# A spectral filter block with a gated FFN on one core: the deferred tiles' half of the last evacuations, moved behind the inverse's first tile

## The chip, the cores and the metric

The kernel runs on one core of one Trainium2 chip. The metric is the device time of one execution in microseconds; several runs are taken and the median is given. The five instruction streams are TensorE (PE, with its weight loads as PEld), VectorE (DVE), ScalarE (ACT), GpSimd (POOL) and SyncE (SP). Each runs its own instructions in order, and they wait for each other by semaphores.

## The reference, cut to what matters

```python
x = A_x                                              # [1, 2048, 576] bf16
X = rfft2(layernorm(x)) * (w_r + 1j * w_i)           # over tokens and channels
h = x + irfft2(X, s=(2048, 576)).astype(bf16)
h2 = h + (gelu(layernorm(h) @ w_gate) * (layernorm(h) @ w_up)) @ w_down
return h2                                            # gate, up: 576x4608, down: 4608x576
```

## The kernel before

The 2048 tokens lie as 16 tiles of 128 tokens (token 16p + c is row p of tile c). The Fourier transforms are matmuls with tables.

**The forward part** handles 16 frequency groups, numbered i = 0 to 15 (GORD gives the place g of each). Its order is the hand-written word list SEQF (L28): D and d are the two passes of the channel transform, B the second token factor, T the multiplication by the filter on DVE, V and v the two passes of the first inverse token factor. The filter's last 32 channels (the remainder) of four groups are put together and go through R and r, q = 0 to 3. `st_V` (L686) evacuates a group's 128x512 results from a PSUM bank pair into V, by ACT and DVE or by one of them (VENG, L29); the last group, V15, is split between both. `st_R` (L702) evacuates the remainders. For q below 3 one copy goes to RB, and eight DMAs, split over SP's and POOL's queues, bring them to their rows in VR. For q = 3, the last, eight copies of 32 partitions x 128 elements write VR directly, four on ACT and four on DVE (L722 to L727). V has the token tile as its third index; VR has it as the last, so the weights of one tile are taken at a step of 16 elements.

**The inverse part** handles 16 token tiles. Tiles 0 to 7 go right away, in the order of the word list SEQ (L35): I and i are the two passes of the inverse channel transform (`i_mm`, L833; V in both, VR in the last step of the second pass), E its evacuation to GS (`i_ev`, L842; letter A, D, P or S for ACT, DVE, POOL or both), N and o the two passes of the last token factor (`n_mm`, L850), a the residual add on DVE (`x_add`, L859), s the sum of squares (L917), q and c the root and the reciprocal (L868, L873), n the normalisation (`norm`, L885, on POOL for tiles 0 to 3), u and U the transposes on PE (L901), e their evacuation, G the first two FFN steps. SEQ begins `I0 I1 I2 i0 E0S i1 E1S i2 E2A N0 I3 o0`. Tiles 8 to 15 are deferred: `def_i` (L991) and `def_n` (L1011) put their matmuls between those of the FFN, from f = 3 on.

**What sets the order.** Each engine's stream is just the order of the calls. PSUM is eight banks, used as four pairs in this stage. A small planner (L813 to L829) walks SEQ and gives each I, N and u the free pair that was used longest ago:

```python
if k in "INu":
    b = min((b for b in range(2 * ing, 4) if b not in held), key=lambda b: last[b])
```

The starting order comes from SEQF: the pair of V15 (banks 4 and 5) and that of R3 (banks 6 and 7) were used last. So I0 and I1 get the two other pairs, I2 that of V15, and N0 that of R3. The class Prog (L190) turns the keys that an operation reads and writes into waits: a matmul into a bank waits for every earlier reader of that bank.

**DMA queues.** SP loads tables, filter rows and the FFN weights; a call of `hold` (L762) lets SP wait for PE's position before a weight load (`loads`, L779: after I0, N0, i3, o1, N3, i7, o3). POOL issues the filter copies, its share of the remainders, and later the FFN weights.

**The FFN** takes four token blocks: 36 steps of gate and up (`gu_part`, L935: 18 matmuls, GELU on ACT, product on DVE), then the down projection (L1042), and the output.

Of the kernel before, what the change touches and what calls it, by code (L numbers as in the profile page):

```python
# [4 lines left out]
BF16 = mybir.dt.bfloat16  # L5
# [26 lines left out]
RENG = ['dve', 'act', 'act', 'act', 'act']  # L32
QR = ((0, 1), (1, 2), (2, 3), (3, 4), (4, 8), (8, 16))
DEF0, DSTEP = 3, 4
SEQ = """I0 I1 I2 i0 E0S i1 E1S i2 E2A N0 I3 o0 i3 N1 I4 o1 a0 E3S N2 o2 a1 s0A q0 i4 a2 s1A I7 c0 N3 E4S q1 s2D i7 I6 o3 E7A i6 c1 N4 o4 a3 q2 E6A c2 N7 I5 o7 a4 n0P N6 s3A a7 i5 n1P n2P q3 c3 o6 u1 U1 u2 E5A u0 U2 a6 n3P e1A e2D U0 N5 u3 e0A o5 a5 U3 G0 e3D G1""".split()  # L35


def _np_bf16(a):
# [8 lines left out]
def build_tables():  # L47
# [7 lines left out]
    T = {}  # L55
# [96 lines left out]
    T["BTAB"] = BN.reshape(128, 2 * 2 * 128)  # L152
    VN = VN.reshape(2, 2, 128, 256)
    assert np.allclose(VN[0, 0], VN[0, 1])
    T["VTAB"] = np.stack([v if k else v.reshape(128, 4, 16, 4).transpose(0, 1, 3, 2).reshape(128, 256) for v, k in ((VN[0, 0], 1), (VN[0, 0], 0), (VN[1, 0], 1), (VN[1, 1], 1), (VN[1, 0], 0), (VN[1, 1], 0))], 1).reshape(128, -1)

    kr = np.arange(1, K2)
    ph2 = ang(np.arange(2 * HK), kr).T
# [173 lines left out]
def _build(nc, A_x, A_w_r, A_w_i, B_w_gate, B_w_up, B_w_down, out):  # L332
# [76 lines left out]
    YS = sb.alloc("YS", [128, NY, 2, KW], BF16)  # L409
    TP = sb.alloc("TP", [128, NZ, 2, 2, 256], BF16)  # L410
    TR = sb.alloc("TR", [128, 2, 2, 2, 128], BF16)
    RB = sb.alloc("RB", [128, 3, 2, 2, 4, NT], BF16)

    GS = sb.alloc("GS", [128, 5, 2, KW], BF16)
    sb.off = v_off
# [14 lines left out]
    P.op(POOL, lambda g: g.memset(EPT[:, :], EPS), w=["EPT"])  # L430
    P.op(POOL, lambda g: g.memset(ZD[:, :], 0.0), w=["ZD"])
    P.op(POOL, lambda g: g.memset(EXQ[:, :], -0.5), w=["EXQ"])
    P.op(POOL, lambda g: g.memset(VR[:, :, :, :, :], 0.0), w=[("V", g, 2 + t) for g in range(NG) for t in range(2)])
    xv = A_x[0].rearrange("(p c) d -> p c d", c=NT)
    ov = out[0].rearrange("(p c) d -> p c d", c=NT)
    tabs = dram["ATAB"].rearrange("p (c k) -> p c k", c=NT)
# [178 lines left out]
    def ev(eng, dst, src, r, w):  # L615
        fn = (lambda v: v.tensor_copy(dst, src)) if eng == DVE else (lambda a: a.activation(dst, src, ACTF.Copy))  # L616
        P.op(eng, fn, r=r, w=w)
# [68 lines left out]
    def st_V(i, second, engs):  # L686
        g, z, b0 = GORD[i], i % NZ, FB["V", i]

        def mm(h, o, ct, first, last, after):
            c, t_ = ct  # L690
            return P.op(PE, lambda t: t.matmul(bank(b0 + o, 0, 128, 128 * c, 128 * c + 128), TP[64 * h:64 * h + 64, z, o, t_, c:256:2], VT[64 * h:64 * h + 64, 0 if g else 2 + o, t_, :],  # L691
                                               start=first, stop=last), r=[("T", z), "VT" if g else "VT2"], w=[("PS", b0 + o)], after=after)

        halves(("V", i), second, [[(c, t_) for c in range(2) for t_ in range(2)]] * 2, mm)
        if not second:
            return
        v5 = V[:, :, :, :, g, :, :].rearrange("p c t n j e -> p j (c t n) e")
        n = 2 // len(engs)
        for a, e in enumerate(engs):
            ev(e, v5[:, n * a:n * a + n], banks(b0 + a, n, 256).rearrange("p a (c e) -> p a c e", e=4), [("PS", b0 + a + k) for k in range(n)], [("V", g, a + k) for k in range(n)])  # L700

    def st_R(q, second):  # L702
        js = range(4 * q, 4 * q + 4)
        b0 = FB["R", q]

        def mm(h, o, pt, first, last, after):
            part, t_ = pt
            return P.op(PE, lambda t: t.matmul(bank(b0 + o, 0, 128, 128 * part, 128 * part + 128), TR[64 * h:64 * h + 64, q % 2, o, t_, :], VT[64 * h:64 * h + 64, 4 + o if part else 1, t_, :], start=first, stop=last),
                        r=[("TR", q % 2, j) for j in range(4)] + ["VT2" if part else "VT1"], w=[("PS", b0 + o)], after=after)

        halves(("R", q), second, [[(part, t_) for part in range(1 + (q == 3)) for t_ in range(2)]] * 2, mm)
        if not second:
            return
        keys = [("PS", b0), ("PS", b0 + 1)]
        if q < 3:
            ev(RENG[q], RB[:, q, :, :, :, :].rearrange("p t o e n -> p o t (e n)"), banks(b0, 2, 128).rearrange("p o (t x) -> p o t x", t=2), keys, [("RB", q)])
            for j, i in enumerate(js):
                for t_ in range(2):
                    k = t_ if q == 2 else (2 * j + t_) % 3 > 0
                    P.dma((SP, POOL)[k], VR[64 * t_ + 32 * (j % 2):64 * t_ + 32 * (j % 2) + 32, GORD[i], :, :, :], RB[32 * j:32 * j + 32, q, t_, :, :, :], f"r{q}{k:d}", r=[("RB", q)], w=[("V", GORD[i], 2 + t_)])  # L720
            return
        for i in js:  # L722
            j, g = i % 4, GORD[i]
            for t_ in range(2):
                dst = VR[64 * t_ + 32 * (j % 2):64 * t_ + 32 * (j % 2) + 32, g, :, :, :].rearrange("p o e n -> p o (e n)")
                src = PS[32 * j:32 * j + 32, b0 * 512:(b0 + 2) * 512].rearrange("p (a c) -> p a c", a=2)[:, :, 128 * (i == LAST) + 64 * t_:128 * (i == LAST) + 64 * t_ + 64]
                ev((ACT, DVE, DVE, ACT)[j], dst, src, keys, [("V", g, 2 + t_)])  # L727

    def dup_w(k, jp, pl=slice(0, 2), eng=None):
        a, b = 64 * jp, 64 - 64 * jp  # L730
# [19 lines left out]
    c = 0  # L750
# [56 lines left out]
    vmain = [("V", g, c) for g in range(NG) for c in range(2)]  # L807
    vtail = [("V", g, c) for g in range(NG) for c in range(2, 4)]
    vk = [vmain, vmain, vtail]
    vkeys = vmain + vtail  # L810


    SLOT, last, held, ing = {}, [sorted(used.values()).index(used[2 * b]) - 4 for b in range(4)], set(), False  # L813
    for t, w in enumerate(SEQ):
        k, i = w[0], int(w[1:].rstrip("ADSP"))
        if k in "INu":
            b = min((b for b in range(2 * ing, 4) if b not in held), key=lambda b: last[b])
            SLOT[k, i] = 2 * b
# [14 lines left out]
    def i_mm(c, second):  # L833
        b, e = SLOT["I", c], ends.setdefault(("I", c), [None, None])
        for j in range(2 + second):
            for r in range(2):
                o, r0 = r ^ (not second), 64 * r
                lhs = V[r0:r0 + 64, j, o, c, :, :, :] if j < 2 else VR[r0:r0 + 64, :, :, :, c].rearrange("p g o e -> p (g o e)")
                e[o] = P.op(PE, lambda t, r0=r0, o=o, j=j, lhs=lhs: t.matmul(bank(b + o, 0, 128, 0, KW), lhs, DT[r0:r0 + 64, 2 * o + j if j < 2 else 4, 0:KW], start=(not second and j == 0), stop=(second and j == 2)),  # L839
                            r=vk[j] + ["DT"], w=[("PS", b + o)], after=[e[o]] if second and j == 0 else [])  # L840

# [118 lines left out]
    def gu_first(i):  # L960
        for a in range(4):
# [2 lines left out]
    P.alias([("ATB", c) for c in range(8)], [("AT", 0), ("AT", 1)])  # L964
    RUN = {"I": lambda c: i_mm(c, False), "i": lambda c: i_mm(c, True), "E": i_ev, "N": lambda c: n_mm(c, False), "o": lambda c: n_mm(c, True), "a": x_add,
           "s": lambda c, e: sq(c, ENG[e]), "q": ln2_q, "c": ln2_c, "n": lambda c, e: norm(c, ENG[e]), "u": lambda c: turn_mm(c, False), "U": lambda c: turn_mm(c, True),
           "e": turn_ev, "G": gu_first}
    for w in SEQ:
        a = w[1:]
        RUN[w[0]](*((int(a[:-1]), a[-1]) if a[-1] in "ADSP" else (int(a),)))  # L970
# [12 lines left out]
        wd_load(j)  # L983


    fdead = ["DT", "IT", "J0", "J1", "ZD"] + [(n_, c) for n_ in ("ATB", "ATS") for c in range(NT)] + [("G", i // 2, i % 2) for i in range(10)] + [*[("Y", a) for a in range(NY)], *[("RB", a) for a in range(3)]]
    fdead += [("T", a) for a in range(NZ)] + [("TR", a, j) for a in range(2) for j in range(4)]
    fnew = ([("AT", f) for f in range(2, 36)] + [("GL", 0), ("GL", 1)] + [("HT", 1, i, k) for i in range(4) for k in range(5)])

# [1 line left out]
    def def_i(c, second):  # L991
        e = ends.setdefault(("X", c), [None, None])
        for j in range(3):
            for r in range(2):
                o, r0 = r ^ (not second), 64 * r
                t_ = j if j < 2 else r
                lhs, rhs = (V[r0:r0 + 64, o, t_, c, :, :, :], DP[r0:r0 + 64, 2 * o + t_, :]) if j < 2 else (VR[r0:r0 + 64, :, :, :, c].rearrange("p g o e -> p (g o e)"), DP[r0:r0 + 64, 4 + o, :])
                e[o] = P.op(PE, lambda t, o=o, t_=t_, lhs=lhs, rhs=rhs, j=j: t.matmul(bank(6 + o, 0, 128, HK * t_, HK * t_ + HK), lhs, rhs, start=(not second and j == 0), stop=(second and j == 2)),  # L998
                            r=vk[o if j < 2 else 2] + ["DP"], w=[("PS", 6 + o)], after=[e[o]] if second and j == 0 else [])
        if not second:  # L1000
            return
        P.op(ACT, lambda a: a.activation(EB[:, :], bank(6, 0, 128, 0, 2 * HK), ACTF.Copy), r=[("PS", 6)], w=["EB"])
# [131 lines left out]
```

## Time and profile before

| | |
|---|---|
| median of 3 runs | 485.22 us (484.98 to 485.22) |
| the profiled execution | 484.82 us |
| span of its trace | 483.0 us, granted TensorE clock 1.000 |
| forward part, last filter matmuls | to about 42.4 us |
| inverse, tiles 0 to 7 | 42.7 to 54.3 us |
| FFN with the deferred tiles among it | 54.3 us to the end |

Times in the trace count from the span's start. In a timeline row stand the start, the length, the engine, the line, the operation with its tiles and shape, and how many instructions it stands for; the brackets give the idle time ahead of it on its engine and what ended that. L616 is the evacuation helper, L242 the DMA helper, so there one goes by the tiles: V, VR and RB as above, GS for E, XO for the residual, HN for the normalised tile. A row of a matmul carries its whole latency, so its length is more than its share of PE.

### The profile page before, as it was taken

What the parts mean: (1) busy time and instruction counts of PE and PEld (TensorE: products, weight loads), DVE (VectorE), ACT (ScalarE), POOL (GpSimd) and SP (SyncE); (2) the same over time, 40 slices, a digit from 0 to 9 for tenths busy, and PEclk for the clock granted to TensorE, in tenths of its full rate; (3) what the DMA queues carried; (4) which work ended last, traced back from release to release, by engine and by line L of the source; (5) the groups of instructions that cost most, each with busy time, mean ns of one, the idle gap of its engine ahead of it and who ended that gap; (6) DMA issues with size and microseconds to landing.
All of it is one profiled execution on the core that took longest, in us unless ns stands there. A gap on an engine that the chain in (4) does not pass through costs nothing.

```text
span 483.0 us, 12887 instructions
## 1 busy us (share of the span) xinstructions
PE 476.7 (99%) x5873; PEld 289.0 (60%) x5874; DVE 183.2 (38%) x366; ACT 145.4 (30%) x291; POOL 51.2 (11%) x86
## 2 busy tenths in 40 slices
PE   7999999999999999999999999999999999999998
PEld 3877755555588644444688544444788444445884
DVE  7998655565500143333200244333101233333011
ACT  6998753434300022332100122233000232223000
POOL 7753317010120000000000000000000000000000
PEclk9999999999999999999999999999999999999999
DMA  8883878951520001000000011000000000000000
GB/s 292 226 219 70 278 248 289 375 104 27 195 88 17 26 18 23 18 1 0 3 14 15 26 24 23 12 0 2 3 14 27 14 1 0 1 1 1 3 26 26
DMA packets 28454, 33.19 MB, mean 69 GB/s; under 512 B 12656, under 2 KB 21488, under 8 KB 28400
## 3 DMA queue, kind: packets, MB, share of 16 engines
q1 hardware_dynamic: 24768, 19.88, 14.6%
q0 software_dynamic: 3632, 12.49, 7.9%
q8 instruction: 46, 0.75, 0.7%
q14 instruction: 8, 0.07, 0.0%
HBM read 26.21 MB, written 2.36 MB: 59 GB/s over the span
## 4 chain that ended last, share of the span: by engine, by line
PE 96%; DVE 1%; DMA 1%; POOL 1%; issue 0%; SPq 0%; POOLq 0%; DVEq 0%
PE PS L948 58%; PE PS L1048 27%; PE PS L650 2%; PE PS L1060 2%; PE PS L691 2%; PE PS L561 1%; DMA XO<-in_A_x_dram 1%; PE PS L670 1%; PE PS L839 1%; PE PS L998 1%; DVE XO L862 1%; PE PS L1015 0%; PE PS L856 0%; POOL XN L577 0%; POOL ATS L530 0%
## 5 line engine op out<-in xcount | busy, mean ns | idle before, releaser
L948 PE MATMUL PS<-HT,WG 64*128 64x512 bf16 (+1 forms) x2142 | 233.4, 372 | 0.1
L948 PEld LDWEIGHTS PS<-HT,WG 64*128 64x128 bf16 x2142 | 109.2, 94 | 111.1 <-DMA WG<-in_B_w_up_dram 0.2
L956 ACT ACTIVATE GL<-PS 128x512 bf16<-128x512 f32 x144 | 85.7, 596 | 281.8 <-PE PS L948 281.8
L957 DVE TENSOR_TENSOR AT<-GL,PS 128x512 bf16<-128x512 bf16 x144 | 98.8, 687 | 166.0 <-ACT GL L956 166.0
L1048 PE MATMUL PS<-WD,AT 64*128 64x288 bf16 x2160 | 133.0, 283 | 0.0
L1048 PEld LDWEIGHTS PS<-WD,AT 64*128 64x128 bf16 x2160 | 107.9, 94 | 25.2
L1035 DVE TENSOR_TENSOR OS<-PS,XO 128x288 bf16<-128x288 f32 (+2 forms) x32 | 13.2, 452 | 125.5 <-PE PS L1048 118.0
L948 PE MATMUL PS<-HT,WGX 64*128 64x512 bf16 x486 | 53.4, 376 | 0.0
L948 PEld LDWEIGHTS PS<-HT,WGX 64*128 64x128 bf16 x486 | 24.3, 94 | 28.2
L865 ACT ACTIVATE OS<-XO,NM 128x576 bf16<-128x576 bf16 x15 | 11.6, 773 | 11.4 <-DVE XO L1019 11.4
L650 PE MATMUL PS<-FT,U 64*128 64x288 bf16 x160 | 13.3, 283 | 0.0
L683 DVE TENSOR_TENSOR TP<-YS,WS 128x1024 bf16<-128x1024 bf16 x16 | 11.0, 686 | 0.9 <-DMA WS<-WS 0.6
L504 DVE BATCH_NORM_STATS2 ST<-XO 128x6 f32<-128x288 bf16 x26 | 10.1, 440 | 2.0 <-DMA XO<-in_A_x_dram 2.0
L691 PE MATMUL PS<-VT,TP 64*128 64x128 bf16 x256 | 10.0, 217 | 0.0
L242 POOL DMA_DIRECT2D WG<-in_B_w_gate_dram x9 | 6.1, 679 | 34.4 <-DMA WG<-in_B_w_gate_dram 31.0
L572 ACT ACTIVATE U<-PS 128x384 bf16<-128x384 f32 (+2 forms) x27 | 9.4, 485 | 0.7 <-PE PS L561 0.7
L561 PE MATMUL PS<-ATS,XO 128*128 128x128 bf16 x96 | 8.1, 219 | 1.5 <-POOL ATS L530 1.5
L242 POOL DMA_DIRECT2D WD<-in_B_w_down_dram x9 | 6.7, 755 | 23.8 <-PE PS L1015 23.8
L616 ACT ACTIVATE CUS<-PS 128x576 bf16<-128x576 f32 x14 | 9.0, 656 | 0.3 <-PE PS L650 0.2
L1060 PE MATMUL PS<-WD,AT 128*128 128x448 bf16 (+1 forms) x72 | 9.0, 286 | 0.0
L616 ACT ACTIVATE YS<-PS 128x576 bf16<-128x576 f32 x14 | 8.9, 657 | 0.3
L691 PEld LDWEIGHTS PS<-VT,TP 64*128 64x128 bf16 x256 | 7.9, 94 | 1.4 <-DVE V L616 0.2
(89 smaller groups left out, 227.9 us busy)
## 6 DMA issues: line engine op xcount, KB each, us to landing
WD<-in_B_w_down_dram POOLq DMA_DIRECT2D x9, 576.0 KB, 12.1
WG<-in_B_w_up_dram SPq DMA_DIRECT2D x6, 576.0 KB, 7.1
WG<-in_B_w_gate_dram POOLq DMA_DIRECT2D x6, 576.0 KB, 6.3
out_dram<-OS SPq DMA_DIRECT2D x30, 72.0 KB, 1.7
XO<-in_A_x_dram SPq DMA_DIRECT2D x6, 288.0 KB, 4.8
WGX<-in_B_w_up_dram SPq DMA_DIRECT2D x2, 576.0 KB, 4.4
WGX<-in_B_w_gate_dram POOLq DMA_DIRECT2D x2, 576.0 KB, 5.5
HT<-HN SPq DMA_TRANSPOSE x60, 2.4
```

The costliest lines, as they stand in the source:

```text
L242: fn = lambda e: e.dma_start(out_ap, in_ap)
L561: P.op(PE, lambda t, b=b, lhs=lhs, p0=p0, p1=p1, s=s, e=e, o=o, c=c: t.matmul(bank(b, p0, p1, o, o + 128), lhs, ATS[:, c, :], start=s, sto ...
L616: fn = (lambda v: v.tensor_copy(dst, src)) if eng == DVE else (lambda a: a.activation(dst, src, ACTF.Copy))
L650: return P.op(PE, lambda t: t.matmul(bank(b0 + o, 0, 128, 0, 2 * HK), U[64 * h:64 * h + 64, us, 2 * i:2 * i + 2, :, :], FT[64 * h:64 * h + ...
L691: return P.op(PE, lambda t: t.matmul(bank(b0 + o, 0, 128, 128 * c, 128 * c + 128), TP[64 * h:64 * h + 64, z, o, t_, c:256:2], VT[64 * h:64 ...
L865: P.op(ACT, lambda a, c=c, out=out: a.activation(out, XO[:, c, 0:D], ACTF.Square, bias=NM[:, c:c + 1], accum_out=SB2[:, 1, c:c + 1]), r=[( ...
L948: op = P.op(PE, lambda t, h0=h0, kt=kt, wt=wt, b=b, s=(not second and j == 0), e=(second and j == n - 1): t.matmul(bank(b, 0, 128, c0, c1) ...
L956: P.op(ACT, lambda a: a.activation(GL[:, s2, :], bank(b0), ACTF.Gelu_apprx_tanh), r=[("PS", b0)], w=[("GL", s2)])
L957: P.op(DVE, lambda v: v.tensor_tensor(AT[:, f, :], GL[:, s2, :], bank(b0 + 1), op=ALU.mult), r=[("GL", s2), ("PS", b0 + 1)], w=[("AT", f)])
L1035: P.op(DVE, lambda v: v.tensor_tensor(OS[:, p % 2, d0:d1], bank(b, 0, 128, 0, d1 - d0), XO[:, c, d0:d1], op=ALU.add), r=[("PS", b), ("X", ...
L1048: e[h] = P.op(PE, lambda t, f=f, h=h, r0=r0, j=j: t.matmul(bank(b0 + h, 0, 128, 0, 288), AT[r0:r0 + 64, f, 128 * p:128 * p + 128], WD[r0:r ...
L1060: P.op(PE, lambda t, b=b, d0=d0, d1=d1, f=f, j=j: t.matmul(bank(b, 0, 128, 0, d1 - d0), AT[:, f, 128 * p:128 * p + 128], WD[:, f, d0:d1], ...
```

## The change

V15's and R3's evacuations are cut in two by token tile: first the half for tiles 0 to 7 (k = 0), later that for the deferred tiles 8 to 15 (k = 1). VR gets the half as its second index, and the table of the remainder's first factor is put in that order, so a remainder's PSUM row holds each half in 32 neighbouring columns per part. V15's second half is the new word `l15` (two copies, ACT and DVE), R3's second half the new word `l3`: two ACT copies to RB and eight DMAs on POOL's queue to VR. SEQ's beginning is reordered, and I2 comes after i0. The planner counts both pairs as held until `l15` and `l3`. The remainders of q below 3 still go in one DMA per group and part, now in two pieces per partition, and SP and POOL take four each of every q (before: SP 3, POOL 5 for q = 0 and 1). The matmuls of the deferred tiles also wait for the late keys.

```diff
-SEQ = """I0 I1 I2 i0 E0S i1 E1S i2 E2A N0 I3 o0 i3 N1 ...
+SEQ = """I0 I1 i0 l15 E0S I2 i1 E1S i2 E2A l3 N0 I3 o0 i3 N1 ...
...
-    VR = sb.alloc("VR", [128, NG, 2, 4, NT], BF16)
+    VR = sb.alloc("VR", [128, 2, NG, 2, 4, NT // 2], BF16)
...
-    RB = sb.alloc("RB", [128, 3, 2, 2, 4, NT], BF16)
+    RB = sb.alloc("RB", [128, 3, 2, 2, 2, 32], BF16)
...
+        if i == LAST:
+            v_half(i, 0, ("V", g))
+            return
...
+    def v_half(i, k, key):
+        for a, e in enumerate((ACT, DVE)):
+            src = bank(FB["V", i] + a, 0, 128, 0, 256).rearrange("p (q x) -> p q x", q=4)[:, :, 32 * k:32 * k + 32].rearrange("p q (n e) -> p q n e", e=4)
+            ev(e, V[:, :, :, 8 * k:8 * k + 8, GORD[i], a, :].rearrange("p c t n e -> p (c t) n e"), src, [("PS", FB["V", i] + a)], [(*key, a)])
...
-                    k = t_ if q == 2 else (2 * j + t_) % 3 > 0
-                    P.dma((SP, POOL)[k], VR[64 * t_ + 32 * (j % 2):64 * t_ + 32 * (j % 2) + 32, GORD[i], :, :, :], RB[32 * j:32 * j + 32, q, t_, :, :, :], f"r{q}{k:d}", r=[("RB", q)], w=[("V", GORD[i], 2 + t_)])
+                    k = t_ ^ (j % 2)
+                    P.dma((SP, POOL)[k], tail_place(i, t_, slice(0, 2)), RB[32 * j:32 * j + 32, q, t_, :, :, :].rearrange("p k o x -> p k (o x)"), f"r{q}{k:d}", r=[("RB", q)], w=[("V", GORD[i], 2 + t_)])
...
-                src = PS[...][:, :, 128 * (i == LAST) + 64 * t_:128 * (i == LAST) + 64 * t_ + 64]
-                ev((ACT, DVE, DVE, ACT)[j], dst, src, keys, [("V", g, 2 + t_)])
+                src = PS[...][:, :, 128 * (i == LAST) + 64 * t_:128 * (i == LAST) + 64 * t_ + 32]
+                ev((ACT, DVE, DVE, ACT)[j], tail_place(i, t_, 0).rearrange("p (o x) -> p o x", o=2), src, keys, [("V", g, 2 + t_)])
...
+    def tail_late(q, engs):
+        b0 = FB["R", 3]
+        for p0, p1, c, e in ((0, 96, 0, engs[0]), (96, 128, 128, engs[1])):
+            ev(ENG[e], RB[p0:p1, 0, :, 1, :, :].rearrange("p t o x -> p o t x"), PS[p0:p1, b0 * 512:(b0 + 2) * 512].rearrange("p (a c) -> p a c", a=2)[:, :, c:c + 128].rearrange("p a (t x) -> p a t x", t=2)[:, :, :, 32:64],
+               [("PS", b0), ("PS", b0 + 1)], [("RB", 0, p0)])
+        for i in range(12, 16):
+            for t_ in range(2):
+                j = i % 4
+                P.dma(POOL, tail_place(i, t_, 1), RB[32 * j:32 * j + 32, 0, t_, 1, :, :].rearrange("p o x -> p (o x)"), "rl", r=[("RB", 0, 96 if i == LAST else 0)], w=[("VL", GORD[i], 2 + t_)])
...
-    SLOT, last, held, ing = {}, [...], set(), False
+    SLOT, last, held, ing = {}, [...], {FB["R", 3] // 2, FB["V", LAST] // 2}, False
...
+        elif k == "l":
+            held.discard(FB["R" if i == 3 else "V", i] // 2)
...
-                lhs = ... VR[r0:r0 + 64, :, :, :, c].rearrange("p g o e -> p (g o e)")
+                lhs = ... VR[r0:r0 + 64, c // 8, :, :, :, c % 8].rearrange("p g o e -> p (g o e)")
...
-                            r=vk[o if j < 2 else 2] + ["DP"], ...
+                            r=(vk[o] if j < 2 else vtail) + vlate + ["DP"], ...
...
+           "l": lambda q: tail_late(q, "AA") if q == 3 else v_half(q, 1, ("VM", GORD[q]))
```

`tail_place` gives the 32 rows of VR that belong to group i and part t_, for one half or for both.

More of the change, by code (lines that the diff above doesn't have):

```diff
@@ L34 @@
 DEF0, DSTEP = 3, 4
-SEQ = """I0 I1 I2 i0 E0S i1 E1S i2 E2A N0 I3 o0 i3 N1 I4 o1 a0 E3S N2 o2 a1 s0A q0 i4 a2 s1A I7 c0 N3 E4S q1 s2D i7 I6 o3 E7A i6 c1 N4 o4 a3 q2 E6A c2 N7 I5 o7 a4 n0P N6 s3A a7 i5 n1P n2P q3 c3 o6 u1 U1 u2 E5A u0 U2 a6 n3P e1A e2D U0 N5 u3 e0A o5 a5 U3 G0 e3D G1""".split()
+SEQ = """I0 I1 i0 l15 E0S I2 i1 E1S i2 E2A l3 N0 I3 o0 i3 N1 I4 o1 a0 E3S N2 o2 a1 s0A q0 i4 a2 s1A I7 c0 N3 E4S q1 s2D i7 I6 o3 E7A i6 c1 N4 o4 a3 q2 E6A c2 N7 I5 o7 a4 n0P N6 s3A a7 i5 n1P n2P q3 c3 o6 u1 U1 u2 E5A u0 U2 a6 n3P e1A e2D U0 N5 u3 e0A o5 a5 U3 G0 e3D G1""".split()
 def _np_bf16(a):
@@ L154, in build_tables @@
     assert np.allclose(VN[0, 0], VN[0, 1])
-    T["VTAB"] = np.stack([v if k else v.reshape(128, 4, 16, 4).transpose(0, 1, 3, 2).reshape(128, 256) for v, k in ((VN[0, 0], 1), (VN[0, 0], 0), (VN[1, 0], 1), (VN[1, 1], 1), (VN[1, 0], 0), (VN[1, 1], 0))], 1).reshape(128, -1)
+    T["VTAB"] = np.stack([v if k else v.reshape(128, 4, 2, 8, 4).transpose(0, 1, 2, 4, 3).reshape(128, 256) for v, k in ((VN[0, 0], 1), (VN[0, 0], 0), (VN[1, 0], 1), (VN[1, 1], 1), (VN[1, 0], 0), (VN[1, 1], 0))], 1).reshape(128, -1)
     kr = np.arange(1, K2)
@@ L432, in _build @@
     P.op(POOL, lambda g: g.memset(EXQ[:, :], -0.5), w=["EXQ"])
-    P.op(POOL, lambda g: g.memset(VR[:, :, :, :, :], 0.0), w=[("V", g, 2 + t) for g in range(NG) for t in range(2)])
+    P.op(POOL, lambda g: g.memset(VR[:, :, :, :, :, :], 0.0), w=[(k, g, 2 + t) for k in ("V", "VL") for g in range(NG) for t in range(2)])
     xv = A_x[0].rearrange("(p c) d -> p c d", c=NT)
@@ L715, in st_R @@
         if q < 3:
-            ev(RENG[q], RB[:, q, :, :, :, :].rearrange("p t o e n -> p o t (e n)"), banks(b0, 2, 128).rearrange("p o (t x) -> p o t x", t=2), keys, [("RB", q)])
+            ev(RENG[q], RB[:, q, :, :, :, :].rearrange("p t k o x -> p o (t k) x"), banks(b0, 2, 128).rearrange("p o (t x) -> p o t x", t=4), keys, [("RB", q)])
             for j, i in enumerate(js):
                 for t_ in range(2):
-                    k = t_ if q == 2 else (2 * j + t_) % 3 > 0
-                    P.dma((SP, POOL)[k], VR[64 * t_ + 32 * (j % 2):64 * t_ + 32 * (j % 2) + 32, GORD[i], :, :, :], RB[32 * j:32 * j + 32, q, t_, :, :, :], f"r{q}{k:d}", r=[("RB", q)], w=[("V", GORD[i], 2 + t_)])
+                    k = t_ ^ (j % 2)
+                    P.dma((SP, POOL)[k], tail_place(i, t_, slice(0, 2)), RB[32 * j:32 * j + 32, q, t_, :, :, :].rearrange("p k o x -> p k (o x)"), f"r{q}{k:d}", r=[("RB", q)], w=[("V", GORD[i], 2 + t_)])
             return
@@ L724, in st_R, with tail_place @@
             for t_ in range(2):
-                dst = VR[64 * t_ + 32 * (j % 2):64 * t_ + 32 * (j % 2) + 32, g, :, :, :].rearrange("p o e n -> p o (e n)")
-                src = PS[32 * j:32 * j + 32, b0 * 512:(b0 + 2) * 512].rearrange("p (a c) -> p a c", a=2)[:, :, 128 * (i == LAST) + 64 * t_:128 * (i == LAST) + 64 * t_ + 64]
-                ev((ACT, DVE, DVE, ACT)[j], dst, src, keys, [("V", g, 2 + t_)])
+                src = PS[32 * j:32 * j + 32, b0 * 512:(b0 + 2) * 512].rearrange("p (a c) -> p a c", a=2)[:, :, 128 * (i == LAST) + 64 * t_:128 * (i == LAST) + 64 * t_ + 32]
+                ev((ACT, DVE, DVE, ACT)[j], tail_place(i, t_, 0).rearrange("p (o x) -> p o x", o=2), src, keys, [("V", g, 2 + t_)])
+    def tail_place(i, t_, k):
+        r0, g = 64 * t_ + 32 * (i % 2), GORD[i]
+        v = VR[r0:r0 + 32, k, g, :, :, :]
+        return v.rearrange("p o e n -> p (o e n)") if k == 0 or k == 1 else v.rearrange("p k o e n -> p k (o e n)")
+    def tail_late(q, engs):
[7 more added lines that the diff above has]
+                P.dma(POOL, tail_place(i, t_, 1), RB[32 * j:32 * j + 32, 0, t_, 1, :, :].rearrange("p o x -> p (o x)"), "rl", r=[("RB", 0, 96 if i == LAST else 0)], w=[("VL", GORD[i], 2 + t_)])
     def dup_w(k, jp, pl=slice(0, 2), eng=None):
@@ L809, in _build @@
     vk = [vmain, vmain, vtail]
-    vkeys = vmain + vtail
-    SLOT, last, held, ing = {}, [sorted(used.values()).index(used[2 * b]) - 4 for b in range(4)], set(), False
+    vlate = [("VM", GORD[LAST], a) for a in range(2)] + [("VL", GORD[i], 2 + t) for i in range(12, NG) for t in range(2)]
+    vkeys = vmain + vtail + vlate
+    SLOT, last, held, ing = {}, [sorted(used.values()).index(used[2 * b]) - 4 for b in range(4)], {FB["R", 3] // 2, FB["V", LAST] // 2}, False
     for t, w in enumerate(SEQ):
@@ L837, in i_mm @@
                 o, r0 = r ^ (not second), 64 * r
-                lhs = V[r0:r0 + 64, j, o, c, :, :, :] if j < 2 else VR[r0:r0 + 64, :, :, :, c].rearrange("p g o e -> p (g o e)")
+                lhs = V[r0:r0 + 64, j, o, c, :, :, :] if j < 2 else VR[r0:r0 + 64, c // 8, :, :, :, c % 8].rearrange("p g o e -> p (g o e)")
                 e[o] = P.op(PE, lambda t, r0=r0, o=o, j=j, lhs=lhs: t.matmul(bank(b + o, 0, 128, 0, KW), lhs, DT[r0:r0 + 64, 2 * o + j if j < 2 else 4, 0:KW], start=(not second and j == 0), stop=(second and j == 2)),
@@ L966, in _build @@
            "s": lambda c, e: sq(c, ENG[e]), "q": ln2_q, "c": ln2_c, "n": lambda c, e: norm(c, ENG[e]), "u": lambda c: turn_mm(c, False), "U": lambda c: turn_mm(c, True),
-           "e": turn_ev, "G": gu_first}
+           "e": turn_ev, "G": gu_first, "l": lambda q: tail_late(q, "AA") if q == 3 else v_half(q, 1, ("VM", GORD[q]))}
     for w in SEQ:
@@ L983, in _build @@
         wd_load(j)
-    fdead = ["DT", "IT", "J0", "J1", "ZD"] + [(n_, c) for n_ in ("ATB", "ATS") for c in range(NT)] + [("G", i // 2, i % 2) for i in range(10)] + [*[("Y", a) for a in range(NY)], *[("RB", a) for a in range(3)]]
+    fdead = ["DT", "IT", "J0", "J1", "ZD"] + [(n_, c) for n_ in ("ATB", "ATS") for c in range(NT)] + [("G", i // 2, i % 2) for i in range(10)] + [*[("Y", a) for a in range(NY)], *[("RB", a) for a in range(3)], ("RB", 0, 0), ("RB", 0, 96)]
     fdead += [("T", a) for a in range(NZ)] + [("TR", a, j) for a in range(2) for j in range(4)]
@@ L996, in def_i @@
                 t_ = j if j < 2 else r
-                lhs, rhs = (V[r0:r0 + 64, o, t_, c, :, :, :], DP[r0:r0 + 64, 2 * o + t_, :]) if j < 2 else (VR[r0:r0 + 64, :, :, :, c].rearrange("p g o e -> p (g o e)"), DP[r0:r0 + 64, 4 + o, :])
+                lhs, rhs = (V[r0:r0 + 64, o, t_, c, :, :, :], DP[r0:r0 + 64, 2 * o + t_, :]) if j < 2 else (VR[r0:r0 + 64, c // 8, :, :, :, c % 8].rearrange("p g o e -> p (g o e)"), DP[r0:r0 + 64, 4 + o, :])
                 e[o] = P.op(PE, lambda t, o=o, t_=t_, lhs=lhs, rhs=rhs, j=j: t.matmul(bank(6 + o, 0, 128, HK * t_, HK * t_ + HK), lhs, rhs, start=(not second and j == 0), stop=(second and j == 2)),
-                            r=vk[o if j < 2 else 2] + ["DP"], w=[("PS", 6 + o)], after=[e[o]] if second and j == 0 else [])
+                            r=(vk[o] if j < 2 else vtail) + vlate + ["DP"], w=[("PS", 6 + o)], after=[e[o]] if second and j == 0 else [])
         if not second:
```

## The prediction, made before the result

> **What bounds the kernel now.** I read the page's busy rows first, then the list of who waited for whom on PE, then the chain of work that ended last, and then the timeline around the hand-over from the forward part to the inverse, where the change lies. Columns of the waits: total us, times, longest.
>
> ```profile
> PE 476.7 (99%) x5873; PEld 289.0 (60%) x5874; DVE 183.2 (38%) x366; ACT 145.4 (30%) x291; POOL 51.2 (11%) x86
> PE PS L839 <- DVE V L616: 0.3, 1, 0.3
> PE PS L839 <- DVE XO L862: 0.2, 1, 0.2
> ```
>
> PE is busy 99% of the span, and only two short waits lie in the inverse (I = L839, N = L856). The first, 0.3 us, is the wait for the last filter group's evacuation, the very thing that the change halves. From the first FFN matmul on, PE runs on with no wait over 0.2 us, so whatever moves that matmul moves the end. What sets it is told by the chain (start, length, engine and line):
>
> ```profile
> 45.86 0.76 DVE XO L862
> 46.62 0.36 DVE GS L845
> 46.98 1.47 DVE XO L862 x2
> 48.45 0.07 DVE RS L875
> 48.52 0.36 DVE GS L845
> 48.88 1.24 DVE OS L922 x2
> 50.12 0.07 DVE RS L875
> 50.19 0.67 DVE XO L862
> 50.91 0.42 PE PS L839 x4
> 54.33 6.35 PE PS L948 x92
> ```
>
> and by the busy time of each engine in three stretches:
>
> ```profile
> core 0: us, PE busy (x) PEld busy (x) DVE busy (x) ACT busy (x) POOL busy (x), PEclk, DMA share, GB/s
> 42.60:45.90 3.30, 3.10 (x47) 2.38 (x48) 2.00 (x7) 2.31 (x7) 0.00 (x0) 1.00 0.41 108
> 45.90:50.90 5.00, 4.68 (x72) 2.93 (x68) 5.00 (x12) 4.11 (x12) 1.46 (x2) 1.00 0.74 196
> ```
>
> From tile 0's residual add (a0, 45.86) to 50.9 the limit is VectorE: 5.00 us busy of 5.00, no gap. PE's waits there do not show as large, but DVE hands it its work. So this stage's price is read at a0: what delays a0 delays PE at 50.91, the first FFN matmul at 54.33, and the end. Before a0, DVE is idle and waits for PE; there PE's own order counts:
>
> ```profile
> 42.16 0.42 DVE L616 CAST V<-PS 128x256 bf16<-128x256 f32 x1
> 42.62 1.19 DVE L616 CAST VR<-PS 32x128 bf16<-32x128 f32 x4
> 42.73 1.16 PE L839 MATMUL PS<-DT,V 64*128 64x288 bf16 x16 [0.34 <-DVE V L616]
> 43.92 0.17 PEld L839 LDWEIGHTS PS<-DT,VR 64*128 64x128 bf16 x2 [0.34 <-issue]
> 44.91 0.42 PE L856 MATMUL PS<-GS,IT 64*128 64x288 bf16 x4
> 45.07 0.65 ACT L616 ACTIVATE GS<-PS 128x576 bf16<-128x576 f32 x1
> 45.86 0.76 DVE L862 TENSOR_TENSOR XO<-PS,XO 128x576 bf16<-128x576 f32 x1 [0.73 <-PE PS L856]
> 46.25 0.41 ACT L846 ACTIVATE GS<-PS 128x288 bf16<-128x288 f32 x1 [0.53 <-PE PS L839]
> ```
>
> 42.73 is I0, 43.92 the first load of remainder weights (VR) for i0, 44.91 is N0, 45.07 is E2A, 45.86 is a0. N0 follows i2 without a gap: its bank pair is free, since R3's evacuation ended at 42.62 + 1.19 = 43.81.
>
> **The change part by part.**
>
> Half evacuations. The prices are in these groups (min/median/max ns):
>
> ```profile
> L616 ACT ACTIVATE V<-PS x13: 378/385/619, 26.3 to 42.2; 128x256 bf16<-128x256 f32 x9, 128x512 bf16<-128x512 f32 x4
> L616 DVE CAST V<-PS x12: 409/416/692, 27.5 to 42.2; 128x256 bf16<-128x256 f32 x9, 128x512 bf16<-128x512 f32 x3
> L616 ACT ACTIVATE VR<-PS x4: 251/266/272, 42.5 to 43.3; 32x128 bf16<-32x128 f32 x4
> L616 DVE CAST VR<-PS x4: 284/286/289, 42.6 to 43.5; 32x128 bf16<-32x128 f32 x4
> ```
>
> 256 elements a partition cost 385 (ACT) and 416 (DVE), 128 cost 266 and 286. V15's first half thus ends 0.13 us earlier and I0 starts at 42.60. By the same slope (0.13 us per 128 elements) a 64-element remainder copy is about 0.21 to 0.22 us: four end near 43.44 instead of 43.81. i0 needs them, and it needs the remainders that came by DMA:
>
> ```profile
> 41.55 0.59 SPq L242 DMA_DIRECT2D VR<-RB  x1
> DMA to landing us min/median/max: 1.8/1.8/1.8
> ```
>
> The last of these lands at 41.55 + 1.8 = 43.35. The VR load follows the last copy by 0.11 now (43.81 to 43.92); so it can come at 43.55 at best, and no later than now if the several waits ahead of it and the landing hold it; I take 43.8. **Gain there: 0.1 of at most 0.37 us.** But only I0 and I1 run ahead of it now, because R3's and V15's bank pairs stay occupied. I2 has V15's pair and waits for l15, which ends at 43.44 + 0.29, plus 0.15 to the matmul (42.58 to 42.73 in the rows): 43.88. With the VR pair ahead I2 starts at 44.0. I2, i1 and i2 are 16 matmuls, 1.16 us by the row of 16: i2 ends at 45.16, and E2A starts at 45.18 where it was 45.07. Half the early gain is given back already.
>
> The deferred remainders (l3). Two ACT copies of 128 elements, 2 x 0.27, in line behind E2A (0.65): the first ends at 45.18 + 0.65 + 0.27 = 46.10, the second at 46.37. Now the step that decides: the planner gives N0 the least recently used pair, which is R3's, before as after; and R3's pair is free only when l3 has read it. PE is in order, so N0, I3, o0 and all behind them stand still until 46.37 + 0.14 = 46.5, against 44.91. a0 comes 0.95 after N0 (45.86 - 44.91; matmuls at PE's own rate): 47.45. **a0 is 1.59 us late.** ACT's gap of 0.53 ahead of 46.25, into which l3's 0.54 seems to fit, hides nothing: the wait is PE's. Idle DVE before a0 grows from 0.73 to some 2 us. Behind a0 DVE had no idle time to give back.
>
> The eight POOL DMAs of l3. Prices and what they stand ahead of:
>
> ```profile
> 39.23 1.96 POOL L242 DMA_DIRECT2D VR<-RB  x4 [0.27 <-ACT RB L616]
> 48.64 0.86 POOL L890 TENSOR_SCALAR HN<-XO,NM,RS 128x640 bf16<-128x640 bf16 x1 [7.45 <-DVE RS L875]
> 48.80 1.31 DVE L922 SCALAR_TENSOR_TENSOR OS<-XO,NM 128x576 bf16<-128x576 bf16 x1
> 51.34 0.87 POOL L890 TENSOR_SCALAR HN<-XO,NM,RS 128x640 bf16<-128x640 bf16 x1 [0.17 <-POOL HN L890]
> 52.54 0.87 POOL L890 TENSOR_SCALAR HN<-XO,NM,RS 128x640 bf16<-128x640 bf16 x1 [0.32 <-DVE RS L875]
> 52.58 0.79 PEld L908 LDWEIGHTS PS<-IDT,HN 64*128 64x128 bf16 x24 [0.18 <-PE PS L908]
> ```
>
> They issue at 0.49 each (1.96 for four), the first 0.27 after ACT's copy, as in the first row: 46.10 + 0.27 + 3.92 = 50.29. Queued behind them is tile 0's normalisation (n0P), which would be due at 48.64 + 1.59 = 50.23. So n0P is held some 0.1 us more; I allow 0.07 to its start and put it at 50.36. Small by itself; but look at s2D (L922, 48.80): 576 elements in 1.31 us, where a0's 576 take 0.76. n0P runs 48.64 to 49.50 beside it, and 49.50 to its end at 50.11 are the 0.61 that 576 elements need. I read this as s2D standing still while n0P reads SBUF, both having SBUF operands. With s2D at 48.80 + 1.59 = 50.39, n0P at 50.36 is still just ahead: s2D ends at 50.36 + 0.86 + 0.61 = 51.83, 1.72 after its old end. **Shift at the end of DVE's run: 1.72.** The Trainium skill, page SBUF — State Buffer, section "SBUF: two separate sides", says that a VectorE operation with two SBUF inputs and a GpSimd operation that reads SBUF share a port pair as an exclusive lock, held for a whole instruction by whichever starts first. The trace agrees (1.31 us). By that rule the order of these two decides 0.6 us, which is the first rival's.
>
> Other parts. The RB copies (128x256) keep their size. Of the 24 remainder DMAs, SP issues 12 instead of 10 and POOL 12 instead of 14; the last four on each are q2's, as before. Each now writes two pieces of 128 bytes a partition; the trace shows no such transfer, so the cost lies between nothing and, doubling one landing of 1.8, 1.8; I take nothing, since the middle group's landing is hidden, and keep 0.3 for the last one, whose cover is only the 0.2 between 43.35 and 43.55. The Trainium skill, page DMA: Bandwidth & Descriptors, section "Why small descriptors are slow (HBM only)", says that transfers between SBUF and SBUF are spared that penalty; by it this term is nil, and no run shows it yet. The VR weights, now at a step of 8 elements for 16, load in 0.14 us against 0.09; PE's matmuls cover them (0.06 each, 16 in 1.16), so between nothing and 48 x 0.045 / 2 = 1.1 us gained; I take nothing. l15's other copies lie in ACT's and DVE's gaps before E0S. The late keys add a wait to the deferred tiles from 60 us on, ten us after the DMAs. One thing is given back:
>
> ```profile
> 58.34 1.84 PEld L948 LDWEIGHTS PS<-HT,WG 64*128 64x128 bf16 x20 [0.19 <-DMA WG<-in_B_w_up_dram]
> ```
>
> PE meets the gate/up weights there 0.1 us too early; those loads are held back by less than PE, so 0.1 is saved.
>
> **Sum:** +1.59 (N0 behind l3, net of the early gain) + 0.13 (n0P, s2D) - 0.1 = **+1.6 us.** On the profiled execution, 484.82 (span 483.0 and 1.8 around it), that is 486.4; the runs' median is 485.22, so I forecast **486.85**.
>
> **The rivals.**
>
> *s2D gets ahead of n0P.* The two are 0.03 us apart in my sum, so a POOL queue slower by 0.1 turns them. Then s2D takes about 0.70 and ends at 51.1, 0.98 late; but n0P waits for it, and n0 to n3 follow each other at 0.87 + 0.17: n2 ends at 54.0 where it ended at 52.21, with at most 0.4 to spare before its transpose (52.58 on), so that path is 1.4 late. Less 0.1: +1.3, **486.5**.
>
> *The landing grows.* If 128-byte pieces land 0.3 later, the VR load is at 44.1 and all behind it 0.3 later: **487.15**. For it: two pieces for one. Against it: 32 small rows on 16 engines.
>
> *Not slower: the stall is not there.* If N0 does not wait on l3 (another bank pair, or copies that run ahead of E2A), PE keeps the two early gains, 0.13 and up to 0.24, and nothing is late; POOL's queue would still put n0P behind s2D, which gives and takes about as much. That is 0 to 0.4 us better: **484.9**. It decides where N0's start is under 45.0. For it: ACT has 0.53 us free just there. Against it: the pair is R3's by the planner's rule, and E2A cannot start before i2 ends. The two early gains are all that the change offers ahead of a0, so a time under 484.5 has no source here.
>
> **How the numbers follow.** Main case 0.52 (486.85), s2D ahead 0.25 (486.5), later landing 0.12 (487.15), no stall 0.08 (484.9), something else 0.03. N0's start is uncertain by 0.2 either way. The range that leaves out the no-stall case and the tails is 486.1 to 487.35. About 0.2%, 0.97 us, is what a measurement of this kernel can tell from no change: slower 0.86, same 0.11, faster 0.03.
>
> **What would show it.** Right: N0's matmuls (first L856) at about 46.5 with a wait on ACT's RB copy; a0 near 47.4; eight POOL DMAs from about 46.4 to 50.3; L922 near 1.4 us; first L948 matmul near 55.9 to 56.0. I0 near 42.6 shows the small gain. Wrong: N0 at 45.0 (then no stall), L922 at 0.7 (then the first rival), or a first L948 matmul before 55.2.

## The result, and the profile after

The changed kernel takes 486.96 us (median of 6 runs, 486.74 to 487.6) against 485.22 us (6 runs, 484.98 to 486.05). The ratio is 1.0036, with a 95% interval of 1.0023 to 1.0049. The profiled execution took 487.11 us, its span is 485.3 us.

PE's waits in the inverse (I is L864 now, N L881, the residual add L887):

```profile
PE PS L881 <- issue: 1.2, 1, 1.2
PE PS L864 <- DVE XO L887: 0.4, 1, 0.4
PE PS L864 <- DVE V L616: 0.3, 1, 0.3
PE PS L864 <- ACT V L616: 0.2, 1, 0.2
```

A wait of 1.2 us at N stands where there was none. "Issue" means that the list finds no releaser for it. The timeline around it shows what PE stood for:

```profile
42.62 0.40 PE L716 MATMUL PS<-VT,TR 64*128 64x128 bf16 x8
43.22 0.91 PE L864 MATMUL PS<-DT,V 64*128 64x288 bf16 x12 [0.21 <-ACT V L616]
44.44 0.17 PEld L864 LDWEIGHTS PS<-DT,VR 64*128 64x128 bf16 x2 [0.62 <-issue]
45.48 0.31 PE L864 MATMUL PS<-DT,VR 64*128 64x288 bf16 x2
45.83 0.65 ACT L616 ACTIVATE GS<-PS 128x576 bf16<-128x576 f32 x1
46.38 0.56 ACT L616 ACTIVATE RB<-PS 96x128 bf16<-96x128 f32 x2
47.04 0.42 PE L881 MATMUL PS<-GS,IT 64*128 64x288 bf16 x4 [1.24 <-issue]
47.99 0.76 DVE L887 TENSOR_TENSOR XO<-PS,XO 128x576 bf16<-128x576 f32 x1 [2.09 <-PE PS L881]
```

i2's last matmuls end at 45.79. E2A runs on ACT from 45.83, l3's two copies (RB) behind it from 46.38 to 46.94, and N0 starts at 47.04. DVE now waits 2.09 us for a0 instead of 0.73. From a0 on it is again without a gap:

```profile
48.00:53.20 5.20, 4.71 (x72) 2.98 (x69) 5.20 (x12) 4.12 (x12) 4.34 (x8) 1.00 0.81 226
```

The columns are those of the stretches before: PE, PEld, DVE (5.20 us busy of 5.20), ACT, POOL. POOL's queue and s2D:

```profile
46.93 3.94 POOL L242 DMA_DIRECT2D VR<-RB  x8 [4.96 <-ACT RB L616]
50.92 0.87 POOL L915 TENSOR_SCALAR HN<-XO,NM,RS 128x640 bf16<-128x640 bf16 x1
50.92 1.49 DVE L947 SCALAR_TENSOR_TENSOR OS<-XO,NM 128x576 bf16<-128x576 bf16 x1
```

The eight DMAs take 3.94 us of POOL's queue; n0P and s2D start together, and s2D takes 1.49 us (1.31 before). The first FFN matmul:

```profile
56.63 6.31 PE PS L973 x92
```

The row of the last filter matmuls (L716) starts at 42.62; the eighth and last of them starts 0.18 later, at 42.80. From there to N0 it is 4.24 us (before 2.73, from 42.18 to 44.91), and to the first FFN matmul 13.83 us (before 12.15). From that matmul on both traces are alike to 0.02 us. **So 1.68 us were lost between the filter part and the FFN, 1.51 of them at N0.** The spans differ by 2.3 us, because this execution's filter part also ended 0.62 us later; the experiments look at that too.

### The profile page after: what moved, and what is told of

Its sections match the earlier page's. It is cut to its first block, busy times and chain, and to the rows that moved or that the text cites. A ratio compares the mean times of both kernels' runs of the same rounds, so it can differ in the third digit from the quotient of the medians.

```text
span 485.3 us, 12901 instructions
## 1 busy us (share of the span) xinstructions
PE 477.8 (98%) x5874; PEld 313.3 (65%) x5874; DVE 183.7 (38%) x367; ACT 145.9 (30%) x294; POOL 54.7 (11%) x92
## 4 chain that ended last, share of the span: by engine, by line
PE 90%; SPq 4%; DMA 2%; DVE 2%; issue 1%; POOL 0%; ACT 0%; DVEq 0%
PE PS L973 58%; PE PS L1073 27%; SPq L242 4%; PE PS L1085 2%; DMA WS<-WS 1%; DMA WS<-in_A_w_r_dram 1%; PE PS L691 1%; PE PS L1023 1%; DVE XO L887 1%; PE PS L864 0%; PE PS L1040 0%; PE PS L881 0%; DVE OS L947 0%; PE PS L670 0%; PE PS L933 0%
## 5 line engine op out<-in xcount | busy, mean ns | idle before, releaser
L973 PEld LDWEIGHTS PS<-HT,WG 64*128 64x128 bf16 x2142 | 119.0, 94 | 101.4 <-DVE AT L982 0.2
L1073 PEld LDWEIGHTS PS<-WD,AT 64*128 64x128 bf16 x2160 | 119.5, 94 | 13.6
L973 PEld LDWEIGHTS PS<-HT,WGX 64*128 64x128 bf16 x486 | 26.9, 94 | 25.6
L650 PE MATMUL PS<-FT,U 64*128 64x288 bf16 x160 | 13.2, 283 | 0.0
L242 POOL DMA_DIRECT2D VR<-RB x20 | 10.3, 522 | 6.0 <-ACT RB L616 6.0
L546 PE MATMUL PS<-ZD 128*128 128x512 bf16 x22 | 7.8, 531 | 1.5 <-POOL ZD L431 1.5
```

Source lines behind the costliest of these rows:

```text
L242: fn = lambda e: e.dma_start(out_ap, in_ap)
L650: return P.op(PE, lambda t: t.matmul(bank(b0 + o, 0, 128, 0, 2 * HK), U[64 * h:64 * h + 64, us, 2 * i:2 * i + 2, :, :], FT[64 * h:64 * h + ...
L973: op = P.op(PE, lambda t, h0=h0, kt=kt, wt=wt, b=b, s=(not second and j == 0), e=(second and j == n - 1): t.matmul(bank(b, 0, 128, c0, c1) ...
L1073: e[h] = P.op(PE, lambda t, f=f, h=h, r0=r0, j=j: t.matmul(bank(b0 + h, 0, 128, 0, 288), AT[r0:r0 + 64, f, 128 * p:128 * p + 128], WD[r0:r ...
```

## The experiments

My theory: PE stands at N0 because R3's bank pair is freed by l3, which waits in line behind E2A; the rest of the loss is s2D meeting n0P. The main rival: the deferral's own work costs the time (two more copies on ACT, eight more DMAs on POOL, twice the pieces). Stage times below are counted from the start of the last filter matmul, and "the stage" is the time from there to the first FFN matmul. Each ratio is against the kernel before, run again on the same chip; its medians there were 485.48, 485.60 and 485.64 us.

**The late half early.** l3 right behind l15, its copies on ACT and DVE:

```diff
-I0 I1 i0 l15 E0S I2 i1 E1S i2 E2A l3 N0
+I0 I1 i0 l15 l3 E0S I2 i1 E1S i2 E2A N0
-           "l": lambda q: tail_late(q, "AA") if q == 3
+           "l": lambda q: tail_late(q, "AD") if q == 3
```

Two more lines of this edit, not shown, make the copies wait for RB's earlier readers and for the copies of R3's first half.

> The changed kernel with l3 moved from behind E2A to right behind l15, and its two copies split between ACT and DVE; all copies, DMAs and pieces stay. Theory (PE stands still at N0 because R3's bank pair is freed by l3, which waits in line behind E2A): N0 follows i2 again without the 1.2 us gap, a0 is within 0.2 us of its old distance from I0, and the time is that of the kernel before, 485.1 to 485.6. Rival (the deferral's own work costs it: two more copies, eight more DMAs on POOL, twice the pieces): nothing of that is gone, so 486.5 or more.

Measured: 485.64 us, ratio 1.0004 (0.9993 to 1.0015). The timeline:

```profile
42.11 0.40 PE L716 MATMUL PS<-VT,TR 64*128 64x128 bf16 x8
43.63 0.27 ACT L616 ACTIVATE RB<-PS 96x128 bf16<-96x128 f32 x1
43.87 0.30 DVE L616 CAST RB<-PS 32x128 bf16<-32x128 f32 x1
44.19 3.92 POOL L242 DMA_DIRECT2D VR<-RB  x8 [3.11 <-ACT RB L616]
45.31 0.44 PE L882 MATMUL PS<-GS,IT 64*128 64x288 bf16 x4
46.28 0.76 DVE L888 TENSOR_TENSOR XO<-PS,XO 128x576 bf16<-128x576 f32 x1 [0.68 <-PE PS L882]
```

N0 follows i2 with no wait, 3.02 us after the last filter matmul, though every copy and all eight DMAs are there. DVE's wait for a0 is 0.68 again. The first FFN matmul comes after 12.46 us. So the stand at N0 came from the place of l3, not from its work, and the rival falls. Of the 0.31 us that are left in the stage, 0.29 stand at N0: the first remainder load came 1.86 us after the last filter matmul (44.15 from 42.29; before 1.74), and I2 goes behind it. In this trace the last remainder DMA was issued at 40.61 and took 3.1 us to land.

**The late half on DVE.** The word list is that of the changed kernel; beside the two lines of waits named above, only the engine of the two copies differs:

```diff
-           "l": lambda q: tail_late(q, "AA") if q == 3
+           "l": lambda q: tail_late(q, "DD") if q == 3
```

> The changed kernel with l3's two copies on DVE instead of ACT, at the same place in the word list. DVE is free after its half of E1S, while ACT has E2A (0.65 us) ahead of them. Theory (N0 stands until l3's copies have read R3's pair, whatever engine makes them): the copies end 0.4 us earlier, N0 comes 3.8 us after the last filter matmul instead of 4.2, and a0 and the first FFN matmul follow by 0.4: some 486.5. Rival (N0 stands for something else, or the deferral's own work costs): 4.2 us and 486.9 as before.

Measured: 486.64 us, ratio 1.0018 (1.0009 to 1.0027).

```profile
45.34 0.60 DVE L616 CAST RB<-PS 96x128 bf16<-96x128 f32 x2
46.09 0.42 PE L882 MATMUL PS<-GS,IT 64*128 64x288 bf16 x4 [0.76 <-DVE RB L616]
```

Here the list names the releaser: N0 waits for the copies to RB. N0 comes after 3.79 us and the first FFN matmul after 13.30. The earlier the copies end, the earlier N0, which follows them by 0.10 us in the changed kernel (46.94 to 47.04) and 0.15 here (45.94 to 46.09).

**Another pair for N0.**

```diff
-E2A l3 N0 I3 o0 i3 N1 I4
+E2A N0 I3 o0 i3 N1 l3 I4
```

> The changed kernel with the word l3 behind N1 instead of ahead of N0: ACT's order is the same, but N0, I3 and N1 get other bank pairs and I4 is the one that waits for R3's. Theory: N0 follows i2, a0 is back, I4 waits some 0.3 us; POOL's eight DMAs still end 1.4 us after n0P is due, so the sum of squares on DVE (s2D) runs ahead of n0P and takes 0.7 instead of 1.3 to 1.5 us, and POOL's n0 to n2 become the limit: some 0.7 us slower than before, 485.9 (485.6 to 486.2). Rival (the deferral's own work): 486.5 or more.

Measured: 487.16 us, ratio 1.0033 (1.0022 to 1.0045). The expectation of the time failed. The front of the stage went as expected: N0 comes after 2.90 us and a0 after 3.94 (before 3.68, changed kernel 5.19), and s2D is ahead of n0P and short:

```profile
50.29 0.81 DVE L947 SCALAR_TENSOR_TENSOR OS<-XO,NM 128x576 bf16<-128x576 bf16 x1
51.61 0.87 POOL L915 TENSOR_SCALAR HN<-XO,NM,RS 128x640 bf16<-128x640 bf16 x1
54.72 0.65 PE L933 MATMUL PS<-IDT,HN 64*128 64x64 bf16 x20 [0.49 <-POOL HN L915]
56.31 0.76 DVE L887 TENSOR_TENSOR XO<-PS,XO 128x576 bf16<-128x576 f32 x1 [0.17 <-PE PS L881]
57.22 0.61 PE L973 MATMUL PS<-HT,WG 64*128 64x256 bf16 x8 [0.88 <-DVE XO L887]
```

Two later waits gave it back, so that the first FFN matmul comes after 13.80 us. The second transposes wait 0.49 us for n2P, queued behind the DMAs, as foreseen. And the planner, with the pairs turned round, gave N5 banks 0 and 1, which the first FFN step writes; so that step waits 0.88 us for the residual add a5, which in the other kernels reads banks 6 and 7. That wait is my edit's, and the time of this run tells nothing of the change; its waits do.

**The new layout alone** (no half evacuations, the old word list):

```diff
-I0 I1 i0 l15 E0S I2 i1 E1S i2 E2A l3 N0
+I0 I1 I2 i0 E0S i1 E1S i2 E2A N0
-        if i == LAST:
-            v_half(i, 0, ("V", g))
-            return
-    ..., {FB["R", 3] // 2, FB["V", LAST] // 2}, False
+    ..., set(), False
```

with R3's eight copies of 128 elements writing both halves of VR and no late keys.

> The kernel before with only the new order of VR and RB (two 128-byte pieces per partition in the remainder DMAs, SP and POOL 12 each, VR weights at a step of 8), nothing deferred and the old word order. Theory: the pieces cost nothing on the path, 485.0 to 485.5, and the last filter matmul ends where it did, near 42.4 us. Rival (the 0.6 us by which the profiled run of the changed kernel reached I0 later is a cost of the pieces and of the new split of the queues): 485.7 to 486.0, and the filter part ends 0.4 to 0.7 us later.

Measured: 485.73 us (11 runs, 484.83 to 487.58), ratio 1.0009 (0.9998 to 1.0020). The stage is 12.14 us to the first FFN matmul, as before: the layout costs nothing there. But the last filter matmul started at 43.80 in this trace, and the interval leaves room for both answers. **Inconclusive** for the filter part.

**Both kernels once more**, for that question.

> The changed kernel once more, for a second trace. Theory: the end of the filter part moves by some tenths of a microsecond to 1.6 from one execution to the next in every kernel, with the landing of the last filter rows; the stage from the last filter matmul to the first FFN matmul is 13.8 us again. Rival (the changed kernel's filter part is always later): the last filter matmul starts at 42.8 us again, against 42.18 in the kernel before.

> The kernel before once more, for a second trace. Theory: the stage from the last filter matmul to the first FFN matmul is 12.1 to 12.3 us again, while the last filter matmul itself may start anywhere from 42.0 to 43.8 us, with the landing of the last filter rows. Rival (only kernels with the new pieces have a late filter part): 42.2 us again.

One execution of each was taken: 487.26 us for the changed kernel, 485.09 us for the kernel before. The stages repeat: 13.80 us in the changed kernel (N0 after 4.22), 12.15 us in the kernel before. The last filter matmul started at 42.97 in the changed kernel and at 42.47 in the kernel before. Over all traces it started, with the old pieces, at 42.18, 42.47 and (in a run below) 42.38; with the new pieces at 42.05, 42.17, 42.29, 42.30, 42.70, 42.80, 42.97, 43.42 and 43.80. The earliest is one with the new pieces, so they do not always cost. The medians show no cost either. In the eight kernels with the new pieces, the median moved against the kernel before by between 0.38 us less and 0.26 us more than the stage in that kernel's (first) trace did: by less in four, by more in three, by the same in one. Whether the pieces make a late end more frequent stays open.

**A ninth DMA** behind l3's eight on POOL's queue, in the changed kernel:

```diff
+        P.dma(POOL, RB[0:32, 1, 0, 1, :, :]..., RB[0:32, 0, 0, 1, :, :]..., "r9", r=[("RB", 0, 0)], w=[("RB", 1)])
```

> The changed kernel with a ninth small DMA on POOL's queue behind l3's eight (it copies 32 rows inside RB, whose target nobody reads). Theory (s2D on DVE stands still while n0P runs on POOL, and which goes first is decided by 0.1 us): n0P now comes 0.5 us after s2D's start, s2D takes 0.7 us, n1P and n2P on POOL become the limit, and the kernel is faster by some 0.3 us than the changed one though it does more: 486.3 to 486.7. Rival (s2D's length has another cause): s2D keeps 1.3 to 1.5 us and the time is that of the changed kernel or up to 0.5 us more, 486.9 to 487.4.

Measured: 487.01 us, ratio 1.0028 (1.0018 to 1.0038); the stage is 13.92 us. Neither side was right:

```profile
50.34 1.35 DVE L948 SCALAR_TENSOR_TENSOR OS<-XO,NM 128x576 bf16<-128x576 bf16 x1
50.82 1.45 POOL L916 TENSOR_SCALAR HN<-XO,NM,RS 128x640 bf16<-128x640 bf16 x1
```

s2D started 0.48 us ahead of n0P and still took 1.35, and n0P took 1.45 instead of 0.87. When the two overlap, both can stretch; a short lead does not save s2D.

**n0P moved out of s2D's way**, in the kernel before, in the kernel with the late half early, and in the changed kernel:

```diff
-a4 n0P N6 s3A a7 i5 n1P n2P q3
+a4 N6 s3A a7 i5 n1P n2P n0P q3
```

> The kernel before with one word moved: n0P stands behind n2P, so POOL takes tiles 1, 2, 0, 3. Theory (s2D on DVE and n0P on POOL hold each other up when they meet): nothing runs on POOL beside s2D, which takes 0.8 instead of 1.31 us; DVE's run ends 0.5 us earlier, tile 0's normalisation is then the late one by some 0.2 us, and the first FFN matmul comes 0.2 to 0.5 us earlier after the last filter matmul (12.15 us before): the time is 0.2 to 0.5 us less, hardly to be told in the timing. Rival (s2D is simply a slow operation): s2D stays at 1.3 us and nothing moves.

> e1 (l3 right behind l15) with n0P behind n2P. Theory: e1's stage from the last filter matmul to the first FFN matmul was 12.46 us; it loses the same 0.2 to 0.5 us and comes to 12.0 to 12.25, the time of the kernel before or 0.1 less. Rival (s2D is simply slow): 12.46 as in e1.

> The changed kernel with n0P behind n2P. Theory (1.5 us of the loss is the stand at N0, the other 0.2 us is s2D's meeting with n0P): the stand stays, s2D takes 0.8 instead of 1.49 us, and the stage from the last filter matmul to the first FFN matmul goes from 13.83 to 13.2 to 13.4 us: 486.4 to 486.6. Rival (POOL's eight DMAs are what costs): POOL is no freer, so 13.8 as before.

s2D takes 0.81 us in all three; the lines of the third:

```profile
50.70 0.81 DVE L947 SCALAR_TENSOR_TENSOR OS<-XO,NM 128x576 bf16<-128x576 bf16 x1
51.70 0.87 POOL L915 TENSOR_SCALAR HN<-XO,NM,RS 128x640 bf16<-128x640 bf16 x1 [1.06 <-DVE RS L900]
```

So s2D was long because of n0P, and the rival that it is simply slow falls. The gain that I expected of it failed twice, though, and came short the third time. The times are 485.36 us, ratio 0.9996 (0.9987 to 1.0005), for the kernel before; 485.52, 0.9994 (0.9985 to 1.0003), with the late half early; 487.01, 1.0029 (1.0019 to 1.0039), for the changed kernel. From a0 to the first FFN matmul it is 8.46 to 8.47 us in all three, as it was in the kernel before (8.47): the 0.5 us that DVE gains are lost at the transposes (L908), which wait for POOL's later normalisations. From the waits of the first:

```profile
PE PS L908 <- POOL HN L890: 0.5, 2, 0.3
```

The whole stage is 12.32 us in the first (the remainder load and N0 came 0.18 later than before, so the move is not what lengthened it) and 12.41 in the second. Only the changed kernel, with 8.64 there, has its 0.18 us back (stage 13.52, where I had expected 13.2 to 13.4). No version here beats the kernel before by what can be measured.

## Why the prediction was right, point by point

- **I0 earlier by 0.13:** I0 starts 0.42 us after the last filter matmul, it was 0.55. Right.
- **The first remainder load earlier by 0.1 of at most 0.37:** it comes at 1.64, it was 1.74 (44.44 from 42.80, 43.92 from 42.18). Right, and the cover that I named is what holds it. The last remainder DMA of SP, in two lines of the trace:

```profile
42.23 0.60 SPq L242 DMA_DIRECT2D VR<-RB  x1
DMA to landing us min/median/max: 1.8/1.8/1.8
```

  It lands at 42.23 + 1.8 = 44.03, and the load follows 0.4 us later; the copies on ACT and DVE were done by 44.02 as well, while in the kernel before the load came 0.11 behind the last copy. The run with the late half early fits: there the copies of R3's first half had ended at 43.51, the last remainder landed at 43.72, and the load came at 44.15, 0.4 behind the landing again. That the landing is what holds the load now was not tried by itself.
- **"The landing grows"** (a rival): 1.8 us before and after for the last one, though each partition's bytes come in two pieces. By the Trainium skill, page DMA: Bandwidth & Descriptors, section "Why small descriptors are slow (HBM only)", it was to be nil between SBUF and SBUF; the trace agrees. Over the nine traces with the new pieces the last landing took 1.8 to 1.9 us in seven; in the two where SP issued it right behind the one before (late half early, ninth DMA) it took 3.1 and 2.7. No run separates the pieces from that order.
- **E2A 0.11 later:** 3.03 for 2.89, so 0.14. I2's matmuls behind the remainder load cost that, as told.
- **N0 behind l3, +1.59:** the step that decided. Measured: +1.51 at N0 and at a0. Two terms made my sum 0.1 too large: E2A's 0.65, of which only 0.55 pass before the next copy starts (45.83 to 46.38), and the 0.14 from the copies to N0, which was 0.10.
- **n0P and s2D, +0.13:** +0.17. n0P and s2D started within the same 0.01 us and s2D stretched to 1.49. That they slow each other is shown by the three runs with n0P moved. What I wrote of the first rival (s2D 0.70 if it gets ahead) is wrong: undisturbed it takes 0.81, and a lead of 0.48 us left it at 1.35. My reading that s2D stands still while n0P runs, and needs 0.61 us after it, was too simple as well: if it stood still it would need its whole 0.81 after n0P, and end 1.51 us after its start in the kernel before, where it took 1.31. About 0.2 us of it pass beside n0P. The Trainium skill, page SBUF — State Buffer, section "SBUF: two separate sides", gives the pair to whichever starts first for a whole instruction; that they collide agrees with the trace, that the first one goes unharmed does not.
- **0.1 back at the gate/up weights:** gained there, but not kept. Counted from the first FFN matmul, the group of 28 FFN matmuls that starts at 61.93 in the kernel before (64.14 in the changed kernel) comes 0.09 us earlier; over the whole way to the end nothing changed by more than 0.02 us. The second trace of the kernel before has that group 0.09 earlier too, so the wait that I counted belonged to one execution. The step of 8 in the VR weights gave nothing either:

```profile
L864 PEld LDWEIGHTS PS<-DT,VR x16: 138/140/143, 44.4 to 54.1; 64*128 64x128 bf16 x16
```

- **Sum:** +1.6 forecast; the stage lost 1.68 (1.65 in the second pair of traces), the medians differ by 1.74. The 0.1 between is within what the filter part's end moves. The mechanism and its main term were right; that the sum is this close is luck in part, since 0.08 too much at N0 stands against 0.04 too little at s2D and the 0.1 that was not kept.

The rival "the stall is not there" had ACT's free 0.53 us ahead of E3S for it. In the run with another pair for N0 the copies did fit into that time: E3S's copy on ACT starts 0.39 us after a0 there, as in the kernel before. But in the changed kernel the bank pair that they held was PE's next one, and no idle time of ACT shortens that.

## What to carry to other kernels

Work that is put off still holds what it reads. Before moving an evacuation, find who gets its buffer next, and place it ahead of that user by the order of the engine that does it: here two copies of 0.27 us made PE stand 1.2 us when they came behind another copy, and not at all when they came ahead of it. And when a stage is set by one engine without a gap, a saving on it counts only if the engine that it hands its work to is not the next to be late (in the kernel before, 0.5 us gained on DVE gave nothing at the end).

## What the runs showed of the hardware that I had not expected

- DVE's s2D (two SBUF inputs, 576 elements) and POOL's normalisation (640 elements), which take 0.81 and 0.87 us apart, took 1.35 and 1.45 us when the first had a lead of 0.48 us. With only DMA issues on POOL beside it (the run with another pair for N0), s2D took 0.81.
- The filter part's end moves by 1.75 us between executions and kernels (42.05 to 43.80), which is as much as this change costs. A stage measured inside the trace repeated to 0.03 us; the whole time needed many runs.
